# A decode layer's first weight transfer, 128 rows in one piece or in pieces of 16 and 112

## The chip, the cores and the metric

The kernel runs on one core of a Trainium2 chip. The metric is the device time of one execution in microseconds (us). Three runs of the kernel before took 526.36, 526.45 and 526.49 us; their median is 526.45 us.

## The reference

One decode step of a layer for a batch of four: a normalisation, then attention over a cached window and a gated feed-forward block side by side, summed with the input.

```python
# B=4, D=640, 32 heads of Dh=192, cache of 8192 positions, W=2048, F=1536, all bf16
xn = layernorm(x)                                    # (4, 1, 640)
q  = (xn @ wq).reshape(4, 1, 32, 192).transpose(...) # wq is (640, 6144)
k, v = k_cache[:, :, -2048:], v_cache[:, :, -2048:]  # the last 2048 positions
p  = softmax(einsum("bhqd,bhkd->bhqk", q, k) * 192**-0.5)
A  = einsum("bhqk,bhkd->bhqd", p, v).reshape(4, 1, 6144) @ wo
B  = (silu(xn @ w1) * (xn @ w3)) @ w2
out = x + A + B
```

The window alone is 32 heads x 2 x 3,072 KB; with the weights the core reads 223 MB, each byte once.

## The kernel before, in words

The program is written out by hand: every engine has its own list of instructions, and semaphores order them. Nothing is scheduled by a planner.

**The load queue.** All loads but that of `x` are issued by SyncE (SP in the profile), in the order of the code. First come the weights of the projections: `wq` in three transfers (L172 to L174), `w1` and `w3` (L176), `w2` (L177). Then come the keys and values, one transfer of 3,072 KB for each head and kind (L160 and L168), two buffers for each kind (`kt0`, `kt1`, `vt0`, `vt1`), and between and behind them the pieces of `wo`. `x` is loaded and the result stored by ScalarE's queue (L335, L359), 4 rows each.

SP waits before some issues. The keys of head h go to the buffer of head h - 2, so their issue waits until VectorE has reduced the first half of that head's scores (`s_red`). The first two value transfers wait until the query projection no longer reads `vt` (`s_pp` 13), because `wq` is kept in the value buffers: its chunks 0 and 1 lie in `vt0`, 2 and 3 in `vt1`, 4 in `prs`. Later value transfers wait for the product with the values two heads before (`s_pv`).

**The rows of `wq`.** `wq` has 640 rows of 6,144 numbers. `wq_v` (the view `"(p kc) n -> p kc n"` with kc = 5) gives partition p the rows 5p to 5p + 4. The first transfer brings rows 5p and 5p + 1: 24,576 bytes that lie together in memory, for each of 128 partitions, 3,072 KB in all. It counts `s_wq0` up by 16 when it has landed.

**The start on the engines.** While `wq` is under way, VectorE and ScalarE normalise `x`, TensorE transposes it (L377) and VectorE spreads it over 128 columns (`xnT`). TensorE then projects: for each half of the 6,144 columns and each of the five chunks it loads `xnT` as the weights (L396) and streams six pieces of 512 columns (matmuls recorded at L370). In front of chunks 0, 2 and 4 of the first half it waits for `s_wq0`, `s_wq1` and `s_wq2`. VectorE and ScalarE copy the queries to `qbc`. The feed-forward block follows on TensorE.

**The heads.** For each head VectorE multiplies the keys by the query (L271, in two halves, into `prs`), TensorE adds the products up in groups (L370 on `prs`), VectorE finishes the sums (L277), a softmax passes over all engines, and TensorE multiplies with the values (L445). At the end TensorE multiplies the heads' results by `wo` (L382) as its last pieces land, two copies bring the sum to `res`, and ScalarE's queue stores it.

## Time and profile before

| what | value |
|---|---|
| median of three runs | 526.45 us |
| time of the profiled execution | 526.31 us |
| its span, first to last instruction | 524.5 us |
| bytes read | 222.96 MB, 425 GB/s over the span |
| SP's load queue | 11,488 packets, 99.0% of 16 engines' time |
| TensorE matmul busy | 364.7 us (70%) |
| VectorE busy | 334.1 us (64%) |
| ScalarE busy | 54.5 us (10%) |
| chain that ended last | 1.1% of the span in all: TensorE 1%, VectorE 0% |
| each issue of L173 | 385 to 418 ns on SP |
| issue to landing, the two transfers of L173 | 9.8 and 16.6 us |

The time of an execution is 1.81 us longer than the span of its instructions. The load queue's share is that of all 16 DMA engines together, so 99.0% says that on the average engine there was a packet for nearly the whole span. A packet here is one row of a transfer (24,576 bytes for the first one), or the 4 bytes with which an engine reports its part of a transfer as landed. The share of a busy engine says little alone, since the engines wait for loads in between.

### The profile page before, as it was taken

The page shows a single profiled execution, that of the slowest core. Times are in us where ns is not written, and L with a number is a line of the kernel's source. Part 1 is how long each engine was busy: PE and PEld are TensorE (multiplying, and loading weights), DVE is VectorE, ACT ScalarE, POOL GpSimd, SP SyncE. Part 2 cuts the span into 40 slices and gives each one's busy share as a digit, 9 for nine tenths or more (in the row PEclk, how much of TensorE's full clock was granted, in tenths as well). Part 3 has the DMA queues.
Part 4 walks back from the last instruction along what each step waited for, and adds up shares of the span by engine and source line. Part 5 has one row for each costly group of instructions (what it writes and reads, how often), then busy time and mean ns, then how long its engine had stood idle before and what let it go on. Part 6 is the DMA issues. An engine that isn't in the chain of part 4 may idle for free. (4 is left out here: it accounts for less than half of the span.)

```text
span 524.5 us, 4777 instructions
## 1 busy us (share of the span) xinstructions
PE 364.7 (70%) x2306; PEld 83.9 (16%) x1553; DVE 334.1 (64%) x286; ACT 54.5 (10%) x175; POOL 3.0 (1%) x16
## 2 busy tenths in 40 slices
PE   2775767676587375876666767687676767687797
PEld 0020101110111011111120112111121112111134
DVE  2136767676367564678776666667776666666871
ACT  2120201010101011011010111110110011111011
POOL 2000000000000000000000000000000000000000
PEclk9887888797878799788797888988788888888799
DMA  8999999999999999999999999999999999999995
GB/s 358 423 439 429 425 437 422 442 427 424 443 427 437 429 428 435 439 427 439 427 439 429 427 439 425 439 429 435 433 427 439 425 440 429 433 435 427 439 419 244
DMA packets 11512, 223.07 MB, mean 425 GB/s; under 512 B 1256, under 2 KB 1392, under 8 KB 2416
## 3 DMA queue, kind: packets, MB, share of 16 engines
q1 hardware_dynamic: 11488, 222.96, 99.0%
q8 instruction: 4, 0.07, 0.0%
q14 instruction: 4, 0.03, 0.0%
q10 hardware_dynamic: 16, 0.01, 0.0%
HBM read 222.96 MB, written 0.01 MB: 425 GB/s over the span
## 5 line engine op out<-in xcount | busy, mean ns | idle before, releaser
L370 PE MATMUL ps<-prs,idb 128*128 128x512 bf16 x768 | 227.7, 459 | 134.6 <-PEq L137 134.6
L271 DVE TENSOR_TENSOR prs<-kt,qbc 128x6144 bf16<-128x6144 bf16 x64 | 214.5, 3353 | 117.6 <-DMA kt<-in_A_k_cache_dram 117.6
L277 DVE TENSOR_REDUCE sc<-ps 128x32 f32<-128x1024 f32 x64 | 77.5, 1211 | 3.1 <-PE ps L370 2.9
L453 PE MATMUL po<-o_sb,sel_w 128*128 128x192 f32 x128 | 49.0, 516 | 0.7 <-PEq L137 0.7
L445 PE MATMUL o_ps<-vt,z 128*8 128x384 bf16 x1024 | 47.2, 326 | 0.1
L348 ACT ACTIVATE gneg<-gmax 1x128 f32<-1x128 f32 x32 | 9.8, 308 | 290.1 <-DVE gmax L286 290.1
L445 PEld LDWEIGHTS o_ps<-vt,z 128*8 128x8 bf16 x1024 | 22.1, 86 | 54.7 <-issue 42.1
L419 PEld LDWEIGHTS <-idb 128*128 128x128 bf16 x64 | 6.3, 98 | 153.3 <-issue 152.8
L453 PEld LDWEIGHTS po<-o_sb,sel_w 128*128 128x128 f32 x128 | 25.6, 223 | 14.3 <-issue 4.9
L355 ACT COPY o_sb<-o_ps 128x384 f32<-128x384 f32 x32 | 15.3, 478 | 117.5 <-PE o_ps L445 117.5
L291 DVE TENSOR_TENSOR z<-ex,mask_b 128x256 bf16<-128x256 bf16 x32 | 13.5, 422 | 19.6 <-ACT ex L352 19.2
L428 PEld LDWEIGHTS mt<-idf,lmax 128*1 128x1 f32 x32 | 3.3, 103 | 117.9 <-issue 117.9
L286 DVE TENSOR_REDUCE gmax<-mt 1x4 f32<-1x128 f32 x32 | 8.9, 277 | 12.7 <-PE mt L428 12.3
L432 PE MATMUL mt<-one,gneg 1*128 1x1 f32 x64 | 11.9, 253 | 4.9 <-PEq L137 4.8
L231 DVE CAST qbc<-ps 128x512 bf16<-128x512 f32 x4 | 2.6, 686 | 20.0 <-PE ps L370 20.0
L437 PEld LDWEIGHTS mt<-rsum,tot_w 128*128 128x128 f32 x64 | 9.6, 191 | 35.1 <-issue 34.7
L370 PE MATMUL ps<-vt,xnT 128*128 128x512 bf16 x31 | 10.7, 480 | 5.5 <-DMA vt<-in_A_wq_dram 4.4
L432 PEld LDWEIGHTS mt<-one,gneg 1*128 1x128 f32 x64 | 9.4, 182 | 23.4 <-issue 23.4
L352 ACT ACTIVATE ex<-sc,negm 128x64 bf16<-128x64 f32 x32 | 11.1, 348 | 1.0
L428 PE MATMUL mt<-idf,lmax 128*1 128x128 f32 x32 | 10.5, 327 | 0.0
L300 DVE TENSOR_SCALAR og<-po,rt 64x192 bf16<-64x192 f32 x16 | 6.6, 413 | 3.8 <-PE po L453 3.6
L350 ACT COPY negm<-mt 128x1 f32<-128x1 f32 x32 | 5.1, 159 | 29.2 <-PE mt L432 29.2
(65 smaller groups left out, 81.9 us busy)
## 6 DMA issues: line engine op xcount, KB each, us to landing
kt<-in_A_k_cache_dram SPq DMA_DIRECT2D x32, 3072.0 KB, 19.6
vt<-in_A_v_cache_dram SPq DMA_DIRECT2D x31, 3072.0 KB, 22.6
vt<-in_A_wq_dram SPq DMA_DIRECT2D x2, 3072.0 KB, 13.2
wt<-in_B_w_dram SPq DMA_DIRECT2D x3, 1920.0 KB, 27.8
wt<-in_A_wo_dram SPq DMA_DIRECT2D x2, 1920.0 KB, 27.8
vt<-in_A_v_cache_dram SPq DMA_DIRECT2D x2, 1536.0 KB, 10.8
kt<-in_A_wo_dram SPq DMA_DIRECT2D x2, 960.0 KB, 14.6
prs<-in_A_wq_dram SPq DMA_DIRECT2D x1, 1536.0 KB, 19.8
```

What stands on the lines that cost most here:

```text
L271: ve.tensor_tensor(out=prs[:, a].rearrange("p q j d -> p (q j) d"), in0=kt[h % 2][:, 2 * a * JQ:2 * (a + 1) * JQ, :], in1=qbc[:, h * Dh:(h ...
L277: ve.tensor_reduce(out=sc[h % 3][:, 2 * a * JQ:2 * (a + 1) * JQ], in_=ps[:, a].rearrange("p q (j d) -> p (q j) d", d=DD), axis=AX.X, op=AL ...
L291: ve.tensor_tensor(out=z[h % 2][:], in0=ex[h % 2][:].unsqueeze(2).to_broadcast([P, NJ, B]), in1=mask_b[:].unsqueeze(1).to_broadcast([P, NJ ...
L348: ae.mul(out=gneg[h % 2][:], in_=gmax[h % 2][:].unsqueeze(1).to_broadcast([1, PB, B]), mul=-SCALE).then_inc(s_gneg, 1)
L352: ae.activation(out=ex[h % 2][:], in_=sc[h % 3][:], func=ACTF.Exp, bias=negm[h % 2][:, 0:1], scale=SCALE, accum_out=rsum[h % 2][:]).then_i ...
L355: ae.copy(out=o_sb[h % 2][:], in_=o_ps[:, 0:2 * Dh]).then_inc(s_osb, 1)
L370: return pe.add_instruction(mybir.InstMatmult(name=nc.get_next_instruction_name(), engine=pe.engine, ins=[pe.lower_ap(rhs), pe.lower_ap(lh ...
L428: pe.transpose(out=mt[0:1, 0:P], in_=lmax[par][:], identity=idf[:]).then_inc(s_tr, 1)
L432: pe.matmul(mt[:, P:P + 1], lhsT=flat(gneg[par]), rhs=one[:], start=True, stop=True).then_inc(s_bc, 1)
L437: m = pe.matmul(mt[:, P + 1:P + 2], lhsT=flat(tot_w[:, par]), rhs=rsum[par][:], start=(par == 0), stop=(par == 1))
L445: m = pe.matmul(o_ps[c * CT:c * CT + 2 * B, 0:2 * Dh].rearrange("p (a d) -> p a d", a=2), lhsT=z[par][:, 2 * jj:2 * jj + 2, :], rhs=vt[par ...
L453: m = pe.matmul(po[:, 0:Dh], lhsT=flat(sel_w[:, par, k]), rhs=o_sb[par][:, k * Dh:(k + 1) * Dh].rearrange("p (r i) -> p i r", i=RPP), star ...
```

## The change

The first transfer of `wq` is issued as two. The first of them covers partitions 0 to 15, the second partitions 16 to 127. Both write the same buffer, `vt0`, with the same bytes as before, and both count `s_wq0`; TensorE's wait in front of chunk 0 is for 32 instead of 16. The transfers behind them and their order stay as they were. On the other engines no instruction is added or moved.

```diff
-    for k0, s in ((0, s_wq0), (2, s_wq1)):
-        sp.dma_start(out=flat(vt[k0 // 2]), in_=wq_v[:, k0:k0 + 2, :].rearrange("p k n -> p (k n)")).then_inc(s, 16)
+    for k0, p0, p1, s in ((0, 0, 16, s_wq0), (0, 16, P, s_wq0), (2, 0, P, s_wq1)):
+        sp.dma_start(out=flat(vt[k0 // 2][p0:p1]), in_=wq_v[p0:p1, k0:k0 + 2, :].rearrange("p k n -> p (k n)")).then_inc(s, 16)
     sp.dma_start(out=wq_rows[4], in_=wq_v[:, 4, :]).then_inc(s_wq2, 16)
...
             if c0 == 0 and kc in (0, 2, 4):
-                pe.wait_ge((s_wq0, s_wq1, s_wq2)[kc // 2], 16)
+                pe.wait_ge((s_wq0, s_wq1, s_wq2)[kc // 2], 16 if kc else 32)
             w = xnT[:, kc].rearrange("p a b -> p (a b)")
```

## The prediction

> **What bounds the kernel now.** I read the page's slices and queues first, then its chain, then the table by stretches for the start and the middle, then SP's issues in order of time.

> From the page, the busy tenths of the 16 DMA engines, SP's load queue (packets, MB, share), and the chain that ended last:

> ```profile
> DMA  8999999999999999999999999999999999999995
> q1 hardware_dynamic: 11488, 222.96, 99.0%
> q10 hardware_dynamic: 16, 0.01, 0.0%
> PE 1%; DVE 0%; issue 0%
> PE acc L382 0%; PE po L453 0%; DVE res L331 0%
> ```

> The DMA engines are full in every slice but the first and the last, and the chain is cut after 1% of the span, where it meets a load. The kernel is one long load: what counts is when the first row starts, and whether any DMA engine ever stands still.

> The table by stretches (stretch, length, busy time and count by engine, TensorE clock, DMA share, GB/s; bytes are booked where a row starts):

> ```profile
> 1.90:2.80 0.90, 0.00 (x0) 0.00 (x0) 0.67 (x5) 0.90 (x1) 0.88 (x3) 1.00 1.72 438
> 2.80:3.40 0.60, 0.00 (x0) 0.00 (x0) 0.57 (x5) 0.00 (x1) 0.47 (x2) 1.00 0.00 0
> 3.40:4.10 0.70, 0.00 (x0) 0.00 (x0) 0.67 (x2) 0.00 (x0) 0.70 (x5) 1.00 1.34 562
> 4.10:4.40 0.30, 0.00 (x0) 0.00 (x0) 0.27 (x2) 0.00 (x0) 0.06 (x1) 1.00 0.00 0
> 4.40:5.10 0.70, 0.00 (x0) 0.00 (x0) 0.38 (x1) 0.28 (x1) 0.00 (x0) 1.00 1.32 562
> ...
> 4.00:518.00 514.00, 361.07 (x2268) 82.06 (x1516) 330.96 (x278) 52.85 (x173) 0.16 (x1) 0.86 1.00 432
> 518.00:520.70 2.70, 2.70 (x30) 1.43 (x30) 0.80 (x2) 0.00 (x0) 0.00 (x0) 1.00 0.40 157
> ```

> 438 GB/s for 0.9 us is 394 KB: sixteen rows of 24,576 bytes, one on each DMA engine. The next sixteen start between 3.4 and 4.1 us, the next between 4.4 and 5.1. So an engine works off one row after the other. From 4 to 518 us the share is 1.00 at 432 GB/s, 27.0 GB/s for each engine: 24,576 bytes in 0.91 us. The trace's packet records say the same closer: 912 ns for nearly all of the 8,320 rows of this size, 9 ns for a 4-byte report, and no gap between the packets of an engine after the first row. Time lost by an engine at the start is never made up, and time won is kept. The last report of a load comes at 520.6 us, and the 3.9 us behind it (last matmuls, copy, store) follow from it.

> SP's issues, and VectorE's first wait for keys:

> ```profile
> 0.96 0.86 SPq L173 DMA_DIRECT2D vt<-in_A_wq_dram  x2
> 31.58 0.54 SPq L168 DMA_DIRECT2D vt<-in_A_v_cache_dram  x1
> 51.88 0.54 SPq L160 DMA_DIRECT2D kt<-in_A_k_cache_dram  x1
> 42.68 6.63 DVE L271 TENSOR_TENSOR prs<-kt,qbc 128x6144 bf16<-128x6144 bf16 x2 [6.27 <-DMA kt<-in_A_k_cache_dram]
> ```

> SP is far ahead of the DMA engines, and VectorE waits 6.27 us for the first keys.

> **The change part by part.** The sum is made against the profiled execution, 526.31 us, which is 0.14 below the median of 526.45.

> *One more issue on SP, and sixteen more reports.* An issue of L173 takes 0.385 to 0.418 us. Everything behind the first moves by 0.4 us on SP, up to the second keys, issued by 5.33 us. Their rows are due only after 42.8 us, and the second `wq` transfer's after 10.8. The engines' backlog hides it: 0 (0.4 if the cover were gone). One more 4-byte report for each engine is 9 ns: 0.01.

> *The start.* The sixteen first rows start between 1.97 and 2.74 us by the packet records, 1.0 to 1.8 after the issue, and end between 3.50 and 4.04; twelve end by 3.78. A transfer of 128 rows seems to be handed to the engines one after the other; with one row for each the late engines should get theirs sooner. The bound is the spread of the starts, 0.77 us of gain; below it nothing, as the early engines' first rows take 1.75 us, 0.8 more than a later row, and an earlier start may only wait longer. I take -0.3, what brings the late engines to the typical 3.7.

> *The first 16 rows.* Here the trace has no row that fits. `x`, 4 rows, went over four engines: the second queue above has 16 packets for two such transfers, a row and a report for each of four. So 16 rows should go one to each of the 16 engines, partition e on engine e. All 128-partition loads run 16 engines at full pace, so the partitions are written over at least 16 paths, eight partitions each on the average. The new first transfer puts all engines on 16 neighbouring partitions. If neighbours don't share a path, it costs no more than a row does now: 0. If eight neighbours are a path, sixteen rows squeeze through two, eight rows in a line: 7 x 0.912 = 6.4 us more. I take four to a path (the other four of the eight elsewhere), the middle of 1, 2, 4, 8 towards its upper end: 3 x 0.912 = 2.74. Against sharing stands that `x`'s four neighbours took 53 ns each at the same time, which is 24 GB/s each; but 5 KB may rest in a buffer on the way. For it stands that rows of every source, weights in order or keys of four batches, have one pace: it seems to be set where they are written.

> [...]

> *The other 112 rows.* Seven for each engine; I take them as neighbours, partitions 16 + 7e to 22 + 7e on engine e. [...] I take 2.5 rows: 2.28. The transfers behind have 128 rows again and give nothing back, since every engine is at its full pace.

> *The wait of 32.* It holds the first projection, which now starts at 10.87 us; behind it on TensorE stand all projections, then the copies on VectorE and ScalarE, and SP's first value issue at 31.58 (`s_pp` 13). The DMA engines have keys to load until 49.9 us, so that issue has 18 us in hand. VectorE's wait of 6.27 us before 42.68 moves along with the keys: 0. Were this cover gone, it would cost the same 5 us, not more.

> Sum: 0.01 - 0.3 + 2.74 + 2.28 = 4.7 us; 526.31 + 4.73 + 0.14 gives 531.2.

> **The rivals.**

> *The engines, not the partitions, set the pace: same.* Then the first row costs what it does now, and only the start counts: 526.45 - 0.3 = 526.15, between 525.7 and 526.9 (0.77 of gain, or 0.4 lost to the second issue). `x`'s 53 ns speak for it. It is also the case where the change doesn't do what it says: if the 16 rows went to the engines that have these partitions today, four each on four engines, and the others began at once with the 112, every engine's sum of rows would be that of today.

> *The 112 rows are dealt out like cards: much slower.* Engine e gets 16 + e, 32 + e and so on, and each of seven waves lies on sixteen neighbours. That is 8 x 2.74 = 21.9 us: 548.0. Nothing in the trace speaks against it, but the 128 rows are evidently not dealt so, at their full pace, if paths are shared at all.

> [...]

> *A faster start: faster.* It decides if the first rows come down from 1.2 to 1.75 us to the 0.912 of all others, because the engines wait there for the handing out of 128 rows. Sixteen rows started at 1.97 would end at 2.88 instead of 4.04 for the last engine: 1.16 us, and 525.3. Against it: the latest starters, with nothing left to hand out behind them, still took 1.2 to 1.3 us.

> **How the numbers follow.** A measurement of this kernel can tell about 0.2% (1.05 us) from no change. Shared paths with neighbouring rows have 0.62, and with what the two pieces can cost their own range is 528.9 (3 rows, 0.3 gained) to 533.1 (7 rows). Same: 0.22. Dealt out: 0.08. The faster start: 0.08. So faster 0.08, same 0.22, slower 0.70. The time is that of the likeliest, 531.2. The range reaches down to the case without sharing, 526.0, and up to 533.1; the dealt rows and the faster start are left out.

> **What would show it.** Right: the sixteen first rows end near 6 to 7 us instead of 3.5 to 4.0; GB/s from 2.8 to 7 us is a fraction of 432; the first projection starts between 13 and 17 instead of 10.87; the engines' reports for `wq0` lie up to 4 us apart, where they are 0.5 apart now; the share is 1.00 again behind it, and all landings up to the end are 3 to 6 us late. A second wave at 3.4 to 4.1 as before would make the sharing wrong, and `wq0` landing by 10.9 the whole forecast. A landing of `wq0` near 32 us would be the dealt rows.

## The result, and the profile after

The changed kernel takes 532.36 us (median of five runs, 532.00 to 532.55) against 526.45 (526.36 to 526.52): 5.91 us more, a ratio of 1.0108 with a 95% interval of 1.0097 to 1.0118. It is slower, as forecast; 532.36 lies inside the forecast's range of 526.0 to 533.1, and 1.2 us above the 531.2 of its sum. The profiled execution took 532.36 us, its span 530.5.

The page after, with the load queue and the rates of the first slices:

```profile
span 530.5 us, 4778 instructions
GB/s 208 372 438 434 439 426 435 421 441 434 427 439 416 444 424 435 434 439 426 435 424 439 435 428 437 425 435 434 432 437 424 435 434 432 439 424 435 430 424 246
q1 hardware_dynamic: 11504, 222.96, 99.0%
```

The first two slices moved 208 and 372 GB/s, where they moved 358 and 423. From the third slice on the rates are about those of before. The queue's share is still 99.0%, with sixteen packets more: the engines were not idle, they were slow.

The table by stretches after:

```profile
1.90:2.80 0.90, 0.00 (x0) 0.00 (x0) 0.67 (x5) 0.89 (x1) 0.88 (x3) 1.00 2.80 438
2.80:3.40 0.60, 0.00 (x0) 0.00 (x0) 0.56 (x4) 0.00 (x0) 0.48 (x2) 1.00 0.00 0
3.40:4.10 0.70, 0.00 (x0) 0.00 (x0) 0.67 (x2) 0.00 (x0) 0.70 (x5) 1.00 0.55 70
4.10:4.40 0.30, 0.00 (x0) 0.00 (x0) 0.27 (x2) 0.00 (x0) 0.07 (x1) 1.00 0.51 82
4.40:5.10 0.70, 0.00 (x0) 0.00 (x0) 0.39 (x1) 0.28 (x1) 0.00 (x0) 1.00 1.98 351
...
7.00:16.00 9.00, 0.71 (x7) 0.35 (x7) 1.18 (x3) 0.16 (x1) 0.00 (x0) 1.00 1.02 276
24.00:524.00 500.00, 354.26 (x2249) 80.53 (x1507) 328.99 (x271) 50.63 (x169) 0.00 (x0) 0.86 1.00 432
```

Bytes and packet times are booked where a row starts, so a share can exceed 1. The sixteen first rows start as before (438 GB/s from 1.9 to 2.8 us). But from 3.4 to 4.1 us only 70 GB/s follow, two rows instead of sixteen. From 7 to 16 us, the time of the 112 rows, the engines are busy all the time (1.02) and move 276 GB/s; a whole transfer before has 431 (from 10.8 to 18.1 us, shown below with the cut by columns). From 24 us to the end it is 432 again. Nothing is given back.

The first projection on TensorE, SP's issues and VectorE's first keys after:

```profile
17.43 1.87 PE L370 MATMUL ps<-vt,xnT 128*128 128x512 bf16 x4 [8.74 <-DMA vt<-in_A_wq_dram]
0.96 1.49 SPq L173 DMA_DIRECT2D vt<-in_A_wq_dram  x3
39.34 0.54 SPq L168 DMA_DIRECT2D vt<-in_A_v_cache_dram  x1
48.99 6.63 DVE L271 TENSOR_TENSOR prs<-kt,qbc 128x6144 bf16<-128x6144 bf16 x2 [4.82 <-DMA kt<-in_A_k_cache_dram]
```

The projection starts 6.56 us later (10.87 before), VectorE's first keys 6.31 later (42.68). Of VectorE's wait for them 4.82 us are left of 6.27, so the cover held. SP issues the first values 7.8 us later, at 39.3 us, but the engines have keys to load until 56.2.

The trace's landing records say it closer. Each engine reports its part of a transfer, so each of these transfers has sixteen reports (us, earliest, median, latest):

| transfer | before | after |
|---|---|---|
| first piece, 16 rows | - | 5.62, 6.29, 6.77 |
| all of chunks 0 and 1 | 10.21, 10.46, 10.73 | 15.95, 16.63, 17.29 |
| chunks 2 and 3 | 17.49, 17.72, 17.99 | 23.51, 23.86, 24.52 |
| keys of head 0 | 42.12, 42.34, 42.66 | 48.02, 48.37, 48.97 |
| last piece of `wo` | 518.70, 519.18, 520.59 | 524.94, 525.33, 526.62 |

The whole loss is there when chunks 0 and 1 have landed: 6.17 us by the median report, 6.14 for chunks 2 and 3, and 6.15 for the last piece of `wo` (6.03 by its latest report).

### The profile page after: what moved, and what is told of

It reads as the page before. It is cut to its first block, busy times and chain, and to the rows that moved or that the text cites. A ratio compares the mean times of both kernels' runs of the same rounds, so it can differ in the third digit from the quotient of the medians.

```text
span 530.5 us, 4778 instructions
## 1 busy us (share of the span) xinstructions
PE 362.8 (68%) x2306; PEld 83.0 (16%) x1553; DVE 334.1 (63%) x286; ACT 54.6 (10%) x175; POOL 3.0 (1%) x16
## 3 DMA queue, kind: packets, MB, share of 16 engines
q1 hardware_dynamic: 11504, 222.96, 99.0%
HBM read 222.96 MB, written 0.01 MB: 420 GB/s over the span
## 5 line engine op out<-in xcount | busy, mean ns | idle before, releaser
L271 DVE TENSOR_TENSOR prs<-kt,qbc 128x6144 bf16<-128x6144 bf16 x64 | 214.5, 3353 | 115.7 <-DMA kt<-in_A_k_cache_dram 115.7
L453 PE MATMUL po<-o_sb,sel_w 128*128 128x192 f32 x128 | 48.9, 516 | 0.7 <-PEq L137 0.7
L453 PEld LDWEIGHTS po<-o_sb,sel_w 128*128 128x128 f32 x128 | 24.9, 216 | 13.3 <-issue 3.1
L370 PE MATMUL ps<-vt,xnT 128*128 128x512 bf16 x31 | 10.8, 481 | 12.9 <-DMA vt<-in_A_wq_dram 11.7
L437 PE MATMUL mt<-rsum,tot_w 128*128 128x1 f32 x64 | 8.1, 231 | 0.0
## 6 DMA issues: line engine op xcount, KB each, us to landing
vt<-in_A_v_cache_dram SPq DMA_DIRECT2D x2, 1536.0 KB, 10.8
```

The lines of the kernel that those rows point to most:

```text
L271: ve.tensor_tensor(out=prs[:, a].rearrange("p q j d -> p (q j) d"), in0=kt[h % 2][:, 2 * a * JQ:2 * (a + 1) * JQ, :], in1=qbc[:, h * Dh:(h ...
L370: return pe.add_instruction(mybir.InstMatmult(name=nc.get_next_instruction_name(), engine=pe.engine, ins=[pe.lower_ap(rhs), pe.lower_ap(lh ...
L437: m = pe.matmul(mt[:, P + 1:P + 2], lhsT=flat(tot_w[:, par]), rhs=rsum[par][:], start=(par == 0), stop=(par == 1))
L453: m = pe.matmul(po[:, 0:Dh], lhsT=flat(sel_w[:, par, k]), rhs=o_sb[par][:, k * Dh:(k + 1) * Dh].rearrange("p (r i) -> p i r", i=RPP), star ...
```

## The experiments

The theory: which partitions a piece has sets its rate, since neighbours share a path on which they are written, four to a path by the prediction's choice, and a piece dealt to the 16 engines in neighbouring shares crowds several engines on one path. That a path has one engine's pace, and that there are therefore 16 of them at least, was the author's inference from the share of 1.00 at 432 GB/s; no trace shows a path, and none shows which rows each engine gets. A whole transfer in neighbouring shares of eight, one row of each share at a time, would be sixteen rows that lie 8 apart; such rows came at 212 GB/s (below), a whole transfer at 431, so by this estimate it is dealt in another way. The rivals: a transfer more, its reports or its place at the start of the program makes the price; rows dealt out in another way; no sharing at all. All medians are set against the kernel before on the same chip.

| kernel | time, us | minus before | ratio, 95% interval |
|---|---|---|---|
| two pieces by columns | 526.86 | 0.4 | 0.9989 to 1.0025 |
| 16 and 112 on the second transfer | 534.30 | 7.8 | 1.0123 to 1.0156 |
| two halves of 64 | 534.10 | 7.6 | 1.0125 to 1.0158 |
| 16, then seven by sevens | 532.87 | 6.4 | 1.0098 to 1.0132 |
| eight of 16 neighbours | 545.37 | 19.0 | 1.0340 to 1.0387 |
| eight of 16, 8 apart | 534.31 | 7.9 | 1.0130 to 1.0189 |
| 16 neighbours more in front | 529.37 | 3.0 | 1.0033 to 1.0067 |
| 16, 8 apart, more in front | 528.31 | 1.9 | 1.0018 to 1.0102 |
| 112 more in front | 536.24 | 9.8 | 1.0163 to 1.0197 |
| seven waves from partition 16 in front | 532.36 | 5.9 | 1.0089 to 1.0123 |
| seven waves from partition 18 in front | 533.10 | 6.6 | 1.0105 to 1.0145 |

**Two pieces by columns.** Undoes the choice of partitions and keeps the second transfer, its reports and the wait for 32.

```diff
-    for k0, s in ((0, s_wq0), (2, s_wq1)):
+    for k0, k1, s in ((0, 1, s_wq0), (1, 2, s_wq0), (2, 4, s_wq1)):
+        sp.dma_start(out=flat(vt[k0 // 2])[:, k0 % 2 * H * Dh:(k1 - k0 // 2 * 2) * H * Dh], in_=wq_v[:, k0:k1, :].rearrange("p k n -> p (k n)")).then_inc(s, 16)
...
-                pe.wait_ge((s_wq0, s_wq1, s_wq2)[kc // 2], 16)
+                pe.wait_ge((s_wq0, s_wq1, s_wq2)[kc // 2], 16 if kc else 32)
```

> The first transfer comes as two again, but each piece has all 128 partitions and half of each row (12,288 bytes). Shared paths: no neighbours are crowded, so the time stays that of before but for 8 ns more for each of 8 rows: 526.5 us, and the first projection starts near 10.9 us. If a second transfer, its 16 more reports or the wait for 32 cost the 5.9 us: 532.4.

526.86 us, ratio 1.0007, no difference that can be told; the interval reaches from 0.6 us less to 1.3 us more. The same stretch of the kernel before and of this one, then this one's first projection in order of time:

```profile
10.80:18.10 7.30, 5.05 (x13) 0.32 (x3) 0.00 (x0) 0.00 (x0) 0.00 (x0) 1.00 1.00 431
10.80:18.10 7.30, 5.05 (x13) 0.28 (x3) 0.00 (x0) 0.00 (x0) 0.00 (x0) 1.00 1.01 433
```

```profile
10.75 1.87 PE L370 MATMUL ps<-vt,xnT 128*128 128x512 bf16 x4 [2.07 <-DMA vt<-in_A_wq_dram]
```

The engines are at 433 GB/s, and the first projection starts at 10.75 us, 0.12 sooner than before. One more transfer, sixteen more reports and the wait cost nothing that shows there. The execution with the trace took 528.48 us, but the keys of head 0 land in it as before (42.35 us by the median report, 42.34 before); what it lost, it lost behind them.

**16 and 112 on the second transfer.** The same cut, at another place; the wait for 32 is now in front of chunk 2.

```diff
+    for k0, p0, p1, st, s in ((0, 0, P, 1, s_wq0), (2, 0, 16, 1, s_wq1), (2, 16, P, 1, s_wq1)):
```

> The first transfer is whole; the second one (chunks 2 and 3 of wq) comes as 16 partitions and 112. Shared paths: the cost goes with the shape and not with the place, so 531 to 533 us as in the changed kernel, with the first projection at 10.9 us and the landing of the second transfer 5 to 6.5 us late. If the cost belongs to the start of the program (cold first rows): within 0.5 us of 526.45.

534.30 us, 7.8 more than before: not a matter of the start, and dearer than there, outside the 531 to 533 expected. Its table by stretches:

```profile
2.80:10.80 8.00, 0.71 (x7) 0.35 (x7) 3.20 (x11) 2.31 (x5) 1.24 (x6) 1.00 1.13 396
10.80:13.40 2.60, 1.42 (x4) 0.10 (x1) 0.00 (x0) 0.00 (x0) 0.00 (x0) 1.00 0.87 132
14.40:24.40 10.00, 2.23 (x7) 0.00 (x0) 0.00 (x0) 0.00 (x0) 0.00 (x0) 0.74 0.98 251
30.00:518.00 488.00, 344.81 (x2140) 75.91 (x1407) 327.57 (x267) 48.69 (x163) 0.00 (x0) 0.85 1.00 431
```

The loss moved to 10.8 to 24.4 us: 132 GB/s under the 16 rows, 251 under the 112. By the median reports the 16 rows came 3.74 us behind the time at which the first transfer lands in the kernel before (10.46), 2.83 more than one row takes, and the 112 rows 10.78 us behind those, 4.40 more than seven rows. The two make 7.2 of the 7.8 us. In the changed kernel the 112 rows lost 3.96 by the same reckoning. The execution with the trace took 536.03 us, 1.7 more than the median; the keys of head 0 land 7.2 us late in it, the last piece of `wo` 9.1, so what it lost beyond came later.

**Two halves of 64.**

```diff
+    for k0, p0, p1, st, s in ((0, 0, 64, 1, s_wq0), (0, 64, P, 1, s_wq0), (2, 0, P, 1, s_wq1)):
```

> The first transfer comes as partitions 0 to 63 and 64 to 127, four neighbours for each engine. [...] If rows were dealt out like cards, 16 neighbours in a wave: 24 rows more, 548.3. If only a piece with one row for each engine is dear: 526.5.

534.10 us: 7.6 more, the time of 8.3 rows of 0.912. It is neither the 548.3 of rows dealt out like cards nor the 526.5 of a price on pieces with one row for each engine. Its stretch:

```profile
6.00:18.00 12.00, 0.71 (x7) 0.35 (x7) 1.18 (x3) 1.15 (x2) 0.00 (x0) 1.00 1.00 215
```

215 GB/s is half of 431, with all engines busy; the two pieces' median reports lie 7.39 us apart, about what 128 rows take in one transfer (7.26 from `wq0` to `wq1` before). 64 partitions came at half the rate of 128.

**Eight pieces of 16, neighbours or 8 apart.** The same number of transfers, rows and bytes; only the choice of partitions differs. The wait in front of chunk 0 is for 8 x 16 = 128.

```diff
+    for k0, p0, p1, st, s in (*((0, 16 * i, 16 * i + 16, 1, s_wq0) for i in range(8)), (2, 0, P, 1, s_wq1)):
...
+    for k0, p0, p1, st, s in (*((0, i, P, 8, s_wq0) for i in range(8)), (2, 0, P, 1, s_wq1)):
```

> The first transfer comes as eight of 16 neighbouring partitions each (0 to 15, 16 to 31, and so on). Shared paths: each piece reaches 4 paths of 16, so its wave of sixteen rows takes four row times; 8 x 3 x 0.912 = 21.9 us more, 548.3. If the number of pieces makes the price and not the partitions: the same time as with eight pieces whose partitions lie 8 apart. No sharing: 526.5 to 527.

> The first transfer comes as eight of 16 partitions that lie 8 apart (0, 8, ... 120, then 1, 9, ...). [...] No sharing: 526.5 to 527.

545.37 and 534.31 us: 19.0 and 7.9 more. Partitions 8 apart cost time too, so it is not next neighbours alone that hold each other up. First the stretch of the neighbours, then that of the ones 8 apart:

```profile
8.00:28.00 20.00, 0.71 (x7) 0.35 (x7) 1.19 (x3) 0.17 (x1) 0.00 (x0) 1.00 0.97 123
```

```profile
6.00:17.00 11.00, 0.71 (x7) 0.35 (x7) 1.18 (x3) 1.15 (x2) 0.00 (x0) 1.00 1.01 212
```

123 against 212 GB/s settles it against the number of pieces: it is which partitions a piece has. With neighbours the engines are busy too (share 0.97); by the packet records each row behind the first sixteen lasts 3.26 us there, where a row has 0.912 in a whole transfer. The reports of successive pieces come every 3.25 us with neighbours and every 1.87 us with partitions 8 apart, 3.6 and 2.05 times 0.912. The neighbours are 2.9 us cheaper than expected, since a wave of sixteen rows took 3.25 us instead of the four row times, 3.65.

In all these runs the addresses that are read change together with the partitions that are written, and no run separates the two. That the reading side is not the cause is argued: `w1`, 1,920 KB in a row in memory, came in one transfer of 128 partitions in 4.58 us (median reports 21.37 and 25.95 in the kernel before), 429 GB/s, while each half of 64 partitions, with its rows spread over twice that length, came at 215. The seven waves from partition 16 and from 18, further below, read at the same spacing, shifted by two partitions, and yet differ in kind.

**16, then seven by sevens.** Spells out the order of rows that the prediction supposed for the 112.

```diff
+    for k0, p0, p1, st, s in ((0, 0, 16, 1, s_wq0), *((0, 16 + i, P, 7, s_wq0) for i in range(7)), (2, 0, P, 1, s_wq1)):
```

> The 16 rows as in the changed kernel; the other 112 come as seven transfers of 16 rows, in which the rows lie 7 partitions apart (16 + j, 23 + j, ... 121 + j). Engine e then writes 16 + 7e + j in turn, which is what I took the transfer of 112 rows to do by itself. If it does, the time is that of the changed kernel, 532.4, within 1 us. If the 112 rows are dealt in another order, the time differs: 529.2 if the order by sevens is free of clashes. If each further transfer had a price of its own (5.9 us), 567.

532.87 us, within the 1 us of the changed kernel's 532.36; the rate from 7 to 16 us is 262 GB/s, beside its 276. So the 112 rows are dealt as neighbours, seven to an engine, or in a way that costs the same. The pieces' reports show each wave (median steps): 1.49, 1.54, 1.05, 1.33, 1.71, 1.52, 1.49 us, 10.1 in all against 6.4 for seven rows alone.

**One piece by itself, in front.** The transfers of before stay whole; one piece more is loaded to `kt1`, and the issue of the keys to `kt1` waits until it is there.

```diff
+    sp.dma_start(out=flat(kt[1][0:16]), in_=wq_v[0:16, 0:2, :].rearrange("p k n -> p (k n)")).then_inc(s_tst, 16)
...
     load_k(0)
+    sp.wait_ge(s_tst, 16)
     load_k(1)
```

> All transfers of the kernel before stay whole; in front of them one more brings 16 neighbouring rows of wq (partitions 0 to 15) to kt1, where the keys of head 1 overwrite them later. The 16-row piece alone is measured, one row for each engine. Shared paths: four row times, 3.65 us more, less up to 0.3 for the earlier start: 529.8 to 530.1. No sharing: one row time, 0.9 more, 527.1 to 527.4.

> The same one more transfer of 16 rows in front, but for partitions 0, 8, ... 120. Shared paths: two row times, 1.82 us more, less up to 0.3: 528.0 to 528.3, 1.8 us less than with neighbouring partitions. No sharing: 527.1 to 527.4, the same as with neighbours.

> All transfers of the kernel before stay whole; in front of them one more brings 112 rows of wq (partitions 16 to 127) to kt1, where the keys of head 1 overwrite them later. The 112-row piece alone is measured, seven rows for each engine, 6.4 us without sharing: 532.8. With the 2.5 rows of the forecast's sum, 8.7 more: 535.1. With what the reports of the changed kernel say of its second piece (10.3 us for seven rows): 536.7.

529.37, 528.31 and 536.24 us: 2.97, 1.91 and 9.75 more than before. Without the rows' own time (1, 1 and 7 times 0.912) that is 2.06, 1.00 and 3.37 us for the crowding, the start included. The stretches of the 16 neighbours and of the 112:

```profile
2.80:6.00 3.20, 0.00 (x0) 0.00 (x0) 2.12 (x8) 1.02 (x3) 1.39 (x6) 1.00 0.65 123
7.00:13.00 6.00, 0.71 (x7) 0.35 (x7) 1.18 (x3) 0.29 (x2) 0.00 (x0) 1.00 0.98 422
```

```profile
3.60:12.50 8.90, 0.71 (x7) 0.35 (x7) 2.44 (x7) 2.31 (x4) 0.56 (x4) 1.00 1.03 287
```

Behind the 16 rows the whole transfer goes at 422 GB/s again, so the piece harms only itself. The 16 rows cost 0.4 to 0.7 us less than expected; the two kernels differ by 1.06 us where 1.8 was expected, but their intervals are 1.7 us or more wide. The 112 rows came out 1.1 us above the forecast's term and 0.5 below what the changed kernel's reports say.

**Seven waves from partition 16 or 18.** The first and the third wave of the sevens took 1.49 and 1.05 us. To see whether all engines wait in such a wave or only some: seven transfers of 16 rows of 12,288 bytes in front, 7 partitions apart and always on the same ones (16, 23, ... 121 with a = 16, or 18, 25, ... 123 with a = 18).

```diff
+    R7 = slice(a, a + 106, 7)
+    for i, t in enumerate((flat(kt[0]), flat(kt[1]), wts[0], wts[1], wts[2], flat(kt[0]), flat(kt[1]))):
+        c = i // 5 * H * Dh
+        sp.dma_start(out=t[R7, c:c + H * Dh], in_=wq_v[R7, 0, :]).then_inc(s_tst, 16)
...
+    sp.wait_ge(s_tst, 112)
     for t, w, s in ((wts[0], B_w1, s_w1), (wts[1], B_w3, s_w3)):
```

> All transfers of the kernel before stay whole; in front of them come seven more, each 16 rows of 12,288 bytes for partitions 16, 23, 30, ... 121, to buffers that later loads overwrite. [...] If a clash holds up all engines, as the reports of the split by sevens suggest (about 1.5 us for a row that takes 0.912 alone): all engines at 5.3 us, reports within 1 us of one another, 531.7.

> [...]

532.36 and 533.10 us. By the times alone the waves from 18, whose rows were the faster ones among the sevens, are 0.7 us the slower. The reports differ in kind. From 16 all sixteen engines go in step, one wave in 0.91 to 0.97 us by the medians, twice the 0.46 of such a row alone (seven at 0.76 were expected, and 531.7 us); the seventh wave's reports lie within 0.63 us. From 18 all but five of the 112 reports are in by 8.52 us, and the last two come at 10.34 and 10.43: most engines are about 1 us ahead of those in the waves from 16, and at least two are 1 us behind. These set the time. So from 16 all engines were held up, from 18 a few. One thing was overlooked: SP needs about 0.62 us for each of these issues, more than 0.46, and the faster waves start out at that pace (0.63 us from the first to the second, 0.81 from the sixth to the seventh). SP's issues of the seven from 16:

```profile
0.95 1.27 SPq L176 DMA_DIRECT2D kt<-in_A_wq_dram  x2
2.27 1.85 SPq L176 DMA_DIRECT2D wt<-in_A_wq_dram  x3
4.16 1.22 SPq L176 DMA_DIRECT2D kt<-in_A_wq_dram  x2
```

Why the one set of partitions holds up all engines and the other only some stays open.

Four neighbours to a path do not account for all the rates. 16 partitions that lie 8 apart, or 64 in a row dealt four to an engine, would by that alone meet on no path, and both came at half the rate (212 and 215 GB/s). Which partitions further apart hold each other up, no run shows.

## Why the prediction came out as it did

**What bounds the kernel: right.** What is lost by 24 us is missing at the end: 6.1 us by the median report when chunks 2 and 3 land, 6.1 at the last piece of `wo`, 5.91 in the medians of the times.

**One more issue, reports and the wait of 32: right at 0.** The cut by columns has all three and is not told from before, within an interval of -0.6 to 1.3 us.

**The start, -0.3: right as far as it can be told.** In the changed kernel the first rows start between 1.98 and 2.47 us by the packet records (1.97 to 2.74 before). A piece of 16 neighbours in the middle takes 3.25 us and in front cost 2.97: 0.28 less. For partitions 8 apart it is 1.87 and 1.91, no gain. The interval of either time is 1.7 us wide or more, so 0.3 can't be told from nothing.

**The first 16 rows, 2.74: right that neighbours cost, near in size.** Together with the start the forecast had 2.44; measured alone it is 2.06. In the middle of the loads it is 2.83 (the second transfer's cut) or 2.34 (3.25 less 0.912, among eight pieces). Four to a path was chosen between 1 and 8 with no row of the trace that showed it; 123 GB/s for 16 neighbours, 1/3.5 of the 431 of a whole transfer, come near it. That 16 partitions 8 apart have 212 and 64 in a row 215 does not follow from it.

**The other 112 rows, 2.28: the term that was too small.** No run shows the 2.5 rows that it was made of; by the reports of the changed kernel the loss is 3.96 us (10.34 less 6.38), 4.3 rows of 0.912, by the piece in front 3.37. The order of the rows was right, or one that costs the same, as the sevens show. What failed is that some engines were to lose much and others little, with the reports of `wq0` up to 4 us apart. In fact even the earliest report of `wq0` came 5.7 us late (15.95 against 10.21), where an engine without a loss under the 112 would have been 2.4 late, and the reports lie 1.34 us apart, those of `wq1` 1.01. The seven waves from 16 show the same with nothing else in the way: all engines kept one pace, 0.93 us for a row of 0.46.

2.06 and 3.96 make 6.0, the loss found. That the forecast came within 1.2 us of the time is in part luck: its first term, with the start, was 0.4 too large where this one was 1.7 too small.

**The signs to look for: three were wrong.** The first rows were to end near 6 to 7 us. By the packet records they end between 3.50 and 5.17, and the second rows start then; but the reports come at 5.62 to 6.77. So the record of such a row ends before its engine reports it landed, and the landing was forecast right, the record was not. The first projection was to start by 17 us and started at 17.43, and the reports of `wq0` lie closer than forecast, both for the term that was too small.

**The range.** Its upper end of 533.1 does not follow from the seven rows that it names: 7 x 0.912 on 526.45 is 532.8. The time lies inside either, 0.5 us below that.

**The rivals.** That the engines set the pace, with `x`'s four rows of 53 ns in its favour, falls with 123 against 212 GB/s; four rows of 1,280 bytes say nothing of 24 KB, and no run shows a buffer on the way. The dealt-out rows fall with 532.9 us for the sevens; eight pieces of neighbours, which are that case spelled out, took 545.4. No run shows more than 0.3 us for the faster start.

## What to carry to other kernels

In this kernel, one unbroken load, the partitions of a transfer mattered more than its size or number: eight pieces of one size went at 123 or 212 GB/s. So cut a load by columns, which cost nothing that could be told here, and not by partitions, which cost 6 us for 3 MB cut at 16 and 7.6 cut in half. A busy share of 1.00 does not say that the DMA engines are at full pace; read the GB/s beside it, here 276 and 431 at shares of 1.02 and 1.00. And take a load's end from its reports, not from its rows' records: for the first 16 rows here 5.62 to 6.77 us against 3.50 to 5.17.
